# Folding the weights' sign into a parametric relu of slope -2^32, in a top-k attention kernel with two feed-forward layers

## The chip, the core and the metric

The program runs on one core of a Trainium2 chip. The metric is the device time of one execution in microseconds (us), lower is better. The core has five engines that work side by side, each through its own queue in a fixed order: PE (TensorE, the matrix multiplier), DVE (VectorE), ACT (ScalarE), POOL (GpSimd) and SP (SyncE), which here only issues DMA transfers. They wait for each other through semaphores. TensorE's clock is granted in two levels, 1.2 and 2.4 GHz; the profile shows it as a share of full speed (0.5 or 1.0, and means between).

## The reference, cut to what matters

```python
# q, k, v: (4, 8, 576, 64) float32
scores = q @ k.T / 8
kth    = 32nd largest of each row                       # top_k = 32
attn   = softmax(where(scores >= kth, scores, -1e9))
x      = (attn @ v), heads side by side                  # (2304, 512)
x = (sigmoid(x @ w_gate) * (x @ w_val)) @ w_out          # 512 -> 1536 -> 512
out = relu(x @ w_in)**2 @ w_out2                         # 512 -> 2048 -> 512
```

The five weight matrices come as 64-bit floats, q, k and v as 32-bit floats.

## The kernel before, in words

**Work.** The 2304 tokens are 18 blocks of 128. Chunks 0 to 5 are one block each, chunks 6 to 11 two blocks. For each chunk the attention runs in units: one block and one head, so 8 units a block and 144 in all. A unit named `_1_4` is block 1, head 4. Its scores are made on PE (`sp`), copied to SBUF by ACT (`S`), ranked on DVE (four MAX8 and three MATCH_REPLACE, `mx` and `W`), turned into weights by ACT (lines 419 and 421 or 435) with small steps on POOL (`bs`, `dg`), transposed on PE (`tp`, `tq`), copied by ACT (`PT`, `PE`), multiplied with the values on PE (`xp`) and, for two heads at a time, copied by ACT into the layers' input (`x_plain` for chunks 0 and 1). When a chunk's four such copies are there, its feed-forward layers run: `pg` (gate and value), `acc` (w_out), `ph` (w_in), `acc` (w_out2). Chunks 0 and 1 run them in plain 32-bit floats (function moe32, lines 907 to 1000); the later ones use two 16-bit halves of each weight and three matmuls for each product.

**Weights.** [...] A weight matrix is cut into raw blocks of 128 rows by 512 columns (`wg_r`, `wv_r`, `wo_r`, `wi_r`, `w2_r`; the page prints the last as `w_r`), each read as pairs of 32-bit words, and two of them make one tile `wg_c`, ..., `w2_c` (printed `w_c`). There are 68 raw blocks in 34 pairs. A 64-bit float's high word holds sign, 11 exponent bits and 20 mantissa bits. Read as a 32-bit float and multiplied by 2^-112 (REBIAS) by ACT at line 619, it has an exponent that fits 8 bits after the shift left by 3 that DVE does at line 621 on the whole pair. The shift pushes the sign out. The low word's top bits are made by ACT at line 625 (`low`), and POOL adds them in at line 635. The sign is put back in one of two ways, by pair: for every third pair (SGN, SGNS) ACT writes it into the low word at line 628 as the sign of a 16-bit float, so that POOL's add carries it in; for the other two thirds DVE takes the sign bit of the high word and ors it into the tile at line 632. That is 24 instructions at line 628 (12 pairs) and 44 at line 632 (22 pairs).

**Order.** No engine's order is written by hand. The program gives each step a priority (a time along an axis: `tw` for weight steps, `ta` for attention, `tm` for the layers) and a scheduler, which keeps its own estimate of durations, sets each engine's order from priorities and dependencies. In the first 120 us the attention of chunks 0 and 1 and the weights' conversion are interleaved on every engine. Raw blocks and converted tiles share a pool of 35 slots (WSLOTS); DMA issues all stand in SP's queue, where a transfer that has to wait for a slot or for a source holds up those behind it.

The lines that the change touches, all of them in conv, and what calls it:

Of the kernel before, what the change touches and what calls it, by code (L numbers as in the profile page):

```python
# [8 lines left out]
F16 = mybir.dt.float16  # L9
BF16 = mybir.dt.bfloat16  # L10
F32 = mybir.dt.float32
# [3 lines left out]
AF = mybir.ActivationFunctionType  # L15
ALU = mybir.AluOpType
# [31 lines left out]
SM2 = ()  # L48
XUP = 1000
DIAG = 2  # L50
SGN = 3
SGNS = (1,)
M4RAW = 0
KEYS1 = 1
GRAM = {2: ("wg",), 3: ("wv",), 5: ("wo",), 9: ("wi",), 13: ("w2",)}
# [3 lines left out]
MUP = 200.0  # L59
WSLOTS = 35  # L60
PREF = 4
YMOD = 0
LOP = 3
LOA = 0
TCI = 6
# [12 lines left out]
def tile_topk_attention__then__two_moe_layers(  # L78
# [14 lines left out]
    nc = tc.nc  # L93
# [464 lines left out]


    REBIAS = float(2.0**-112)  # L560
    weights = {"wg": w_gate, "wv": w_val, "wo": w_out, "wi": w_in, "w2": w_out2}
    order = ["wg", "wv", "wo", "wi", "w2"]
    pairs_of = {}
# [4 lines left out]
    raws = {}  # L568
    fetched = [0]
    live = [0]  # L570
    nblk = [0]
    flat = {}
    sums = {}
    parts = {}
# [3 lines left out]
    def fetch_to(i):  # L578
        while fetched[0] < len(blocks):
            b = fetched[0]  # L580
            spare = b >= len(blocks) - M4RAW
            if b > i and not (b <= i + PREF and (spare or live[0] + 3 <= WSLOTS)):
                break
            n, kt, fb = blocks[b]
            src = weights[n][kt * P : (kt + 1) * P, fb * 512 : (fb + 1) * 512]
            pool, kw = (mpool, {"tag": "m4", "bufs": M4}) if spare else (wpool, {"tag": "w"})
            if src.dtype == F32:
                t = pool.tile([P, 512], F32, name=f"{n}_r{kt}_{fb}", **kw)
                nc.sync.dma_start(t, src)
            else:  # L590
                t = pool.tile([P, 512, 2], U32, name=f"{n}_r{kt}_{fb}", **kw)
                nc.sync.dma_start(t.rearrange("p f t -> p (f t)"), src.bitcast(U32))
            if not spare:
                live[0] += 1
            raws[(n, kt, fb)] = t
            fetched[0] += 1

    def conv(name, pi):

        pr = pairs_of[name][pi]  # L600
        fetch_to(blocks.index((name, *pr[-1])))
        if (name, pi) in CM4:
            c = mpool.tile([P, 2, 512], F32, tag="m4", bufs=M4, name=f"{name}_c{pi}")
        else:
            c = wpool.tile([P, 2, 512], F32, tag="w", name=f"{name}_c{pi}")
            live[0] += 1
        rs = [raws.pop((name, kt, fb)) for kt, fb in pr]
        ci = c.bitcast(U32)
        wide = weights[name].dtype != F32
        for e, r in enumerate(rs):  # L610
            nblk[0] += 1
            if not wide:
                nc.gpsimd.tensor_copy(c[:, e], r)
            elif YMOD and nblk[0] % YMOD == 0:
                nc.gpsimd.tensor_scalar(
                    c[:, e], r.bitcast(F32)[:, :, 1], REBIAS, 1.0, op0=ALU.mult, op1=ALU.mult
                )
            else:
                nc.scalar.activation(c[:, e], r.bitcast(F32)[:, :, 1], AF.Copy, scale=REBIAS)
        if wide:  # L620
            nc.vector.tensor_scalar(ci, ci, 3, None, op0=ALU.logical_shift_left)
            for e, r in enumerate(rs):
                hi = r[:, :, 1]
                low = r[:, :, 0].bitcast(I32)
                nc.scalar.activation(low, r[:, :, 0], AF.Copy, scale=float(2.0**-29))
                if nblk[0] // 2 % SGN in SGNS:

                    nc.scalar.activation(
                        r.bitcast(F16)[:, :, 1], hi.bitcast(F32), AF.Copy, scale=float(2.0**-60)
                    )  # L630
                else:
                    nc.vector.scalar_tensor_tensor(
                        ci[:, e], hi, 0x80000000, ci[:, e], op0=ALU.bitwise_and, op1=ALU.bitwise_or
                    )
                nc.gpsimd.tensor_tensor(
                    c.bitcast(I32)[:, e], c.bitcast(I32)[:, e], low, op=ALU.add
                )
        live[0] -= sum(blocks.index((name, *b)) < len(blocks) - M4RAW for b in pr)
        for e, (kt, fb) in enumerate(pr):
            flat[(name, kt, fb)] = (c, e)  # L640
# [43 lines left out]
    def weight_step(n=1):  # L684
        for _ in range(min(n, len(steps) - nstep[0])):
            name, pi = steps[nstep[0]]
            conv(name, pi)
            nstep[0] += 1
# [649 lines left out]
```

## Time and profile before

| | us |
|---|---|
| median of 3 runs | 1262.75 |
| lowest, highest run | 1257.21, 1265.05 |
| the profiled execution, own time | 1259.55 |
| its span, first to last instruction | 1257.6 |
| PE busy in the span | 1164.5 (93%) |
| DVE, POOL, ACT busy | 951.2, 845.8, 832.5 |

The page has one execution. Its span begins with the first instruction; 1.95 us of its own time lie outside. PE is busy 93% of the span, but the 40 slices of the page are not alike: PE's share is low in the first tenth and near full from then on, while ACT, DVE and POOL are busiest in that first tenth. So the views have to be read by stretch, and the stretch from about 33 us, where the weights' conversion begins, to about 120 us, where chunk 0's layers begin, is told apart from the rest.

### The profile page before, as it was taken

The page shows a single profiled execution, that of the slowest core. Times are in us where ns is not written, and L with a number is a line of the kernel's source. Part 1 is how long each engine was busy: PE and PEld are TensorE (multiplying, and loading weights), DVE is VectorE, ACT ScalarE, POOL GpSimd, SP SyncE. Part 2 cuts the span into 40 slices and gives each one's busy share as a digit, 9 for nine tenths or more (in the row PEclk, how much of TensorE's full clock was granted, in tenths as well). Part 3 has the DMA queues.
Part 4 walks back from the last instruction along what each step waited for, and adds up shares of the span by engine and source line. Part 5 has one row for each costly group of instructions (what it writes and reads, how often), then busy time and mean ns, then how long its engine had stood idle before and what let it go on. Part 6 is the DMA issues. An engine that isn't in the chain of part 4 may idle for free. (4 is left out here: it accounts for less than half of the span.)

```text
span 1257.6 us, 30621 instructions
## 1 busy us (share of the span) xinstructions
PE 1164.5 (93%) x11477; PEld 949.1 (75%) x11477; DVE 951.2 (76%) x1965; ACT 832.5 (66%) x1719; POOL 845.8 (67%) x1294
## 2 busy tenths in 40 slices
PE   7653999999989979999999999999999999999998
PEld 5543887897877967878788778877886887787775
DVE  5998889789989988998899879998889969210010
ACT  4999987577878767876777766776567657323122
POOL 1698765467888577886877887787678659515233
PEclk9655999999999989999999999999999999999999
DMA  6988872123445466664677574656434523300000
GB/s 168 341 310 268 263 251 78 46 73 92 117 139 137 111 129 153 156 126 100 139 166 142 127 163 106 152 119 146 85 69 98 120 54 59 55 2 1 18 1 17
DMA packets 243188, 153.92 MB, mean 122 GB/s; under 512 B 193120, under 2 KB 209504, under 8 KB 243040
## 3 DMA queue, kind: packets, MB, share of 16 engines
q1 hardware_dynamic: 243040, 151.97, 48.2%
q8 instruction: 90, 1.47, 0.5%
q14 instruction: 58, 0.48, 0.1%
HBM read 105.51 MB, written 18.09 MB: 98 GB/s over the span
## 5 line engine op out<-in xcount | busy, mean ns | idle before, releaser
L393 DVE MAX8 mx<-W 128x8 f32<-128x576 f32 x432 | 327.7, 759 | 10.6
L394 DVE MATCH_REPLACE8 W<-mx,W 128x576 f32<-128x576 f32 x288 | 213.9, 743 | 0.0
L863 PE MATMUL ph<-x,wi_w 128*128 128x256 f16 (+1 forms) x1920 | 190.7, 253 | 7.3 <-ACT x L837 5.8
L884 PE MATMUL acc<-w_w,rh 128*128 128x512 f16 x768 | 182.2, 379 | 0.3 <-POOL rh L876 0.3
L863 PEld LDWEIGHTS <-wi_w 128*128 128x128 f16 x1920 | 156.7, 99 | 32.7 <-issue 8.3
L758 PE MATMUL pg<-xs,wg_w 128*128 128x256 f16 (+1 forms) x1440 | 147.4, 252 | 0.0
L758 PE MATMUL pv<-xs,wv_w 128*128 128x256 f16 (+1 forms) x1440 | 141.3, 251 | 2.6 <-DVE th L770 1.5
L382 PE MATMUL sp<-kst,qt 128*128 128x288 f32 x608 | 129.0, 326 | 12.4 <-DMA kst<-ks 7.4
L465 POOL TENSOR_TENSOR pp<-S,pp 128x512 f16<-128x512 f32 x192 | 137.1, 736 | 1.9
L419 ACT ACTIVATE S<-S,mx 128x576 f32<-128x576 f32 x144 | 111.8, 776 | 33.4 <-DVE mx L393 32.5
L758 PEld LDWEIGHTS <-wg_w 128*128 128x128 f16 x1440 | 117.8, 98 | 17.0 <-issue 0.7
L770 DVE TENSOR_TENSOR th<-pv,th 128x512 f32<-128x512 f32 (+1 forms) x60 | 34.7, 578 | 125.3 <-PE pv L758 118.1
L798 PEld LDWEIGHTS <-wo_w 128*128 128x128 f16 x1440 | 117.7, 98 | 14.6 <-issue 2.5
L758 PEld LDWEIGHTS <-wv_w 128*128 128x128 f16 x1440 | 117.1, 98 | 15.4 <-issue 3.4
L884 PEld LDWEIGHTS <-rh 128*128 128x128 f16 x768 | 72.3, 98 | 72.4 <-POOL rh L876 0.5
L385 ACT COPY S<-sp 128x576 f32<-128x576 f32 x144 | 92.0, 639 | 46.4 <-PE sp L382 39.9
L393 DVE MAX8 mx<-S 128x8 f32<-128x576 f32 x144 | 107.3, 745 | 20.1 <-ACT S L385 20.0
L463 POOL TENSOR_SCALAR S<-S,bs 128x576 f32<-128x576 f32 x96 | 71.9, 748 | 58.9 <-ACT pp L462 58.5
L394 DVE MATCH_REPLACE8 W<-mx,S 128x576 f32<-128x576 f32 x144 | 106.9, 742 | 0.0
L382 PEld LDWEIGHTS sp<-kst,qt 128*128 128x128 f32 x608 | 89.8, 192 | 21.8 <-DMA kst<-ks 7.5
L798 PE MATMUL acc<-gh,wo_w 128*128 128x256 f16 (+1 forms) x1104 | 104.6, 247 | 1.0 <-POOL gh L774 0.9
L875 POOL TENSOR_TENSOR r<-r 128x512 f32<-128x512 f32 (+1 forms) x80 | 70.2, 878 | 51.5 <-ACT rh L874 50.5
(246 smaller groups left out, 2315.5 us busy)
## 6 DMA issues: line engine op xcount, KB each, us to landing
kst<-ks SPq DMA_DIRECT2D x112, 288.0 KB, 3.1
v<-vd SPq DMA_DIRECT2D x32, 320.0 KB, 3.2
qn<-in_q_dram SPq DMA_DIRECT2D x128, 64.0 KB, 2.3
wi_r<-in_moe_w_in_dram SPq DMA_DIRECT2D x16, 512.0 KB, 7.0
w_r<-in_moe_w_out_dram SPq DMA_DIRECT2D x16, 512.0 KB, 5.2
v<-in_v_dram SPq DMA_DIRECT2D x56, 128.0 KB, 2.5
wg_r<-in_moe_w_gate_dram SPq DMA_DIRECT2D x12, 512.0 KB, 6.0
wv_r<-in_moe_w_val_dram SPq DMA_DIRECT2D x12, 512.0 KB, 6.3
```

The costliest lines, as they stand in the source:

```text
L382: nc.tensor.matmul(sp[:, e, 0:HALF], l, r, start=(x == 0), stop=(x == len(ops) - 1))
L385: nc.scalar.copy(ss.rearrange("p (e s) -> p e s", e=2), sp[:, :, 0:HALF])
L393: return nc.vector.max(m8, st.cur).ins
L394: ins = nc.vector.match_replace(st.wk, m8, st.cur, NEG).ins
L419: nc.scalar.activation(wk, wk, AF.Prelu, bias=kth, scale=-1.0, alpha=1.0 / BIG)
L463: nc.gpsimd.tensor_scalar(wk, wk, rz, 1.0, op0=ALU.mult, op1=ALU.mult)
L465: nc.gpsimd.tensor_tensor(pp[:, o : o + e - f], wk[:, f:e], pp[:, f:e], op=ALU.subtract)
L758: nc.tensor.matmul(pp[:, e * N : (e + 1) * N], wblk(wd, a, c, f0, P), xs[:, b_, c, :], start=(e == 0 and n == 0), stop=(n == 3 * KM - 1), ...
L798: nc.tensor.matmul(accs[d // 2][:, (d % 2) * N : (d % 2 + 1) * N], wblk("wo", a, f, d * P, P), gh[:, b_, e * N : (e + 1) * N], start=(f == ...
L863: nc.tensor.matmul(ph[:, e * N : (e + 1) * N], wblk("wi", a, c, f0, P), x2[:, b_, c, :], start=(e == 0 and n == 0), stop=(n == 3 * KM - 1) ...
L875: nc.gpsimd.tensor_tensor(r, r, r, op=ALU.mult)
L884: nc.tensor.matmul(acc2[i][:, 0:DM], gh[:, b_, e * N + i * P : e * N + (i + 1) * P], wblk("w2", a, f, 0, DM), start=(f == 0 and x == 0), s ...
```

## The change

ACT's scaling at line 619 becomes a parametric relu: for a negative input the result is multiplied by -2^32 as well. The value is then positive, and its exponent is larger by 32, which is one more bit above the eight that the shift keeps; the shift left by 3 carries that bit to the place of the sign. So the sign comes through the shift, and both ways of putting it back, lines 628 and 632, are gone. The numbers of instructions at lines 619, 621, 625 and 635 stay. An unused way of scaling on POOL (YMOD, which was 0) goes too.

```diff
-SGN = 3
-SGNS = (1,)
...
     REBIAS = float(2.0**-112)
+    NEGBIT = -float(2.0**32)
...
         for e, r in enumerate(rs):
-            nblk[0] += 1
             if not wide:
                 nc.gpsimd.tensor_copy(c[:, e], r)
-            elif YMOD and nblk[0] % YMOD == 0:
-                nc.gpsimd.tensor_scalar(
-                    c[:, e], r.bitcast(F32)[:, :, 1], REBIAS, 1.0, op0=ALU.mult, op1=ALU.mult
+            else:
+                nc.scalar.activation(
+                    c[:, e], r.bitcast(F32)[:, :, 1], AF.Prelu, scale=REBIAS, alpha=NEGBIT
                 )
-            else:
-                nc.scalar.activation(c[:, e], r.bitcast(F32)[:, :, 1], AF.Copy, scale=REBIAS)
         if wide:
             nc.vector.tensor_scalar(ci, ci, 3, None, op0=ALU.logical_shift_left)
             for e, r in enumerate(rs):
-                hi = r[:, :, 1]
                 low = r[:, :, 0].bitcast(I32)
                 nc.scalar.activation(low, r[:, :, 0], AF.Copy, scale=float(2.0**-29))
-                if nblk[0] // 2 % SGN in SGNS:
-
-                    nc.scalar.activation(
-                        r.bitcast(F16)[:, :, 1], hi.bitcast(F32), AF.Copy, scale=float(2.0**-60)
-                    )
-                else:
-                    nc.vector.scalar_tensor_tensor(
-                        ci[:, e], hi, 0x80000000, ci[:, e], op0=ALU.bitwise_and, op1=ALU.bitwise_or
-                    )
                 nc.gpsimd.tensor_tensor(
                     c.bitcast(I32)[:, e], c.bitcast(I32)[:, e], low, op=ALU.add
                 )
```

Since a scheduler sets the order, the other instructions move as well. Lines after the change are smaller by up to 17: 619 becomes 611, 625 becomes 618, 552 becomes 549, 964 becomes 948.

ACT's queue ahead of the copy that completes chunk 0's input (`x_plain<-xp_0_3`, the last heads of block 0), before:

```order
L486 COPY PT_0_7_943<-tp_0_7_944 128x512
L495 COPY PE_0_3_855<-tq_0_7_950 64x128
L619 ACTIVATE wi_c0_1000<-wi_r0_0_890 128x512
L628 ACTIVATE wi_r0_0_890<-wi_r0_0_890 128x512
L619 ACTIVATE wi_c0_1000<-wi_r1_0_892 128x512
L625 ACTIVATE wi_r1_0_892<-wi_r1_0_892 128x512
L619 ACTIVATE wi_c1_1080<-wi_r2_0_982 128x512
L625 ACTIVATE wi_r2_0_982<-wi_r2_0_982 128x512
L419 ACTIVATE S_1_2_936<-S_1_2_936,mx_1_2_1060 128x576
L628 ACTIVATE wi_r1_0_892<-wi_r1_0_892 128x512
L552 COPY x_plain_324<-xp_0_3_953 128x128
```

and the same place now:

```order
L483 COPY PT_0_7_909<-tp_0_7_910 128x512
L492 COPY PE_0_3_825<-tq_0_7_916 64x128
L611 ACTIVATE wi_c0_964<-wi_r0_0_858 128x512
L618 ACTIVATE wi_r0_0_858<-wi_r0_0_858 128x512
L611 ACTIVATE wi_c0_964<-wi_r1_0_860 128x512
L618 ACTIVATE wi_r1_0_860<-wi_r1_0_860 128x512
L611 ACTIVATE wi_c1_1042<-wi_r2_0_948 128x512
L618 ACTIVATE wi_r2_0_948<-wi_r2_0_948 128x512
L549 COPY x_plain_318<-xp_0_3_919 128x128
```

The two sign steps are gone and line 419's step for unit `_1_2` stands earlier; in the whole queue ahead of this copy there are 39 scalings in both orders, and 14 sign steps before and none now.

SP's queue where the second weight matrix (`wv`) is fetched, before:

```order
L592 DMA wv_r2_0_462<-in_moe_w_val_dram 128x1024
L592 DMA wv_r3_0_464<-in_moe_w_val_dram 128x1024
L592 DMA wv_r0_1_476<-in_moe_w_val_dram 128x1024
L155 DMA kn_1_0_726<-in_k_dram 128x4x64 x2
L592 DMA wv_r1_1_478<-in_moe_w_val_dram 128x1024
```

and now:

```order
L589 DMA wv_r2_0_452<-in_moe_w_val_dram 128x1024
L589 DMA wv_r3_0_454<-in_moe_w_val_dram 128x1024
L152 DMA kn_1_0_700<-in_k_dram 128x4x64 x2
L589 DMA wv_r0_1_464<-in_moe_w_val_dram 128x1024
L589 DMA wv_r1_1_466<-in_moe_w_val_dram 128x1024
```

One weight block (`wv_r0_1`) has gone behind the fetch of keys `kn_1_0`, which waits for a slot that PE frees.

PE's queue where chunk 0's second layer begins (`ph_0_0`, on w_in), before:

```order
L939 MATMUL acc1_0_1261<-g_0_5_1672,wo_c5_986 128x128 x8
L483 MATMUL tp_1_6_1968<-dg_1_6_1934,S_1_6_1541 128x128 x4
L382 MATMUL sp_2_2_2109<-kst_2_2_0_1951,qt_2_1_0_1963 128x288
L494 MATMUL tq_1_6_1975<-dg_1_6_1934,S_1_6_1541 64x128
L964 MATMUL ph_0_0_1810<-x_plain_324,wi_c0_1000 128x128 x2
```

and now:

```order
L541 MATMUL xp_1_1_1508<-PE_1_1_1384,v_1_1_0_725 64x128 x2
L339 MATMUL qpt_2_0_1764<-ident_81,qn_2_0_1481 128x128 x2
L948 MATMUL ph_0_0_1742<-x_plain_318,wi_c0_964 128x128 x2
L948 MATMUL ph_0_0_1742<-x_plain_318,wi_c1_1042 128x128 x2
...
L948 MATMUL ph_0_1_1799<-x_plain_318,wi_c0_964 128x128 x2
L948 MATMUL ph_0_1_1799<-x_plain_318,wi_c1_1042 128x128 x2
L480 MATMUL tp_1_4_1772<-dg_1_4_1535,S_1_4_1116 128x128 x4
```

Chunk 0's second layer stands ahead of the transposes of units `_1_4` to `_1_6` and the scores of units `_2_0` to `_2_2`, which it followed before. From the first `pg` of chunk 2 on, PE's order is the one before but for a unit here and there.

## Rows read from the trace of the kernel before

**Rows 1.** Busy time by stretch: start, length, engines, granted clock, DMA share, GB/s.
```profile
32.00:63.00 31.00, 20.14 (x98) 15.25 (x96) 28.25 (x52) 29.96 (x53) 20.56 (x21) 0.63 0.94 340
33.00:120.00 87.00, 43.52 (x212) 33.52 (x211) 80.34 (x136) 83.75 (x149) 70.67 (x65) 0.58 0.86 306
...
126.00:157.00 31.00, 28.42 (x287) 26.15 (x287) 25.60 (x53) 29.17 (x55) 22.92 (x24) 1.00 0.81 264
...
283.00:1069.00 786.00, 759.14 (x8333) 619.52 (x8333) 698.26 (x1481) 561.56 (x1226) 601.92 (x1016) 0.99 0.54 120
```

**Rows 2.** PE's waits, 33 to 120 us: total, times, longest.
```profile
PE tp L483 <- DVE kn L176: 15.0, 1, 15.0
PE tp L483 <- ACT x_plain L552: 6.8, 3, 3.2
```

**Rows 3.** PE's waits, 126 to 1069 us.
```profile
PE sp L382 <- DMA kst<-ks: 7.4, 8, 1.7
PE acc L939 <- DVE g L929: 4.2, 2, 2.1
```

**Rows 4.** ACT and PE in order of time: start, duration, idle time before.
```profile
33.32 1.35 ACT L628 ACTIVATE wg_r<-wg_r 128x512 f16<-128x512 f32 x1
34.42 0.72 ACT L625 ACTIVATE wg_r<-wg_r 128x512 int32<-128x512 uint32 x1
...
118.70 1.34 ACT L628 ACTIVATE wi_r<-wi_r 128x512 f16<-128x512 f32 x1
120.07 0.27 ACT L552 COPY x_plain<-xp 128x128 f32<-128x128 f32 x1
...
122.31 2.34 PE L917 MATMUL pg<-x_plain,wg_c 128*128 128x128 f32 x10
```

**Rows 5.** ACT's sign steps alone (line 628), two stretches.
```profile
33.00:126.00 93.00, 18.95 (x14) 0.58 0.86 304
126.00:220.00 94.00, 13.40 (x10) 0.98 0.62 197
```

**Rows 6.** DVE's sign steps alone (line 632), the same stretches.
```profile
33.00:126.00 93.00, 19.53 (x26) 0.58 0.86 304
126.00:220.00 94.00, 11.69 (x18) 0.98 0.62 197
```

**Rows 7.** ACT's groups: busy, mean ns; idle before.
```profile
L419 ACT ACTIVATE S<-S,mx 128x576 f32<-128x576 f32 x144 | 111.8, 776 | 33.4 <-DVE mx L393 32.5
L462 ACT ACTIVATE pp<-S,bs 128x576 f16<-128x576 f32 x96 | 74.5, 776 | 42.9 <-issue 20.3 <-DVE bs L458 16.4 <-ACT qn L357 1.9
...
L619 ACT ACTIVATE wi_c<-wi_r 128x512 f32<-128x512 f32 x16 | 10.9, 685 | 0.1
```

**Rows 8.** POOL's adds (line 635), 33 to 120 us.
```profile
33.00:120.00 87.00, 54.38 (x37) 0.58 0.86 306
```

**Rows 9.** POOL and DVE in order of time.
```profile
33.63 0.30 POOL L416 TENSOR_SCALAR bs<-mx 128x1 f32<-128x1 f32 x1 [5.70 <-DVE mx L393]
...
41.03 2.54 POOL L635 TENSOR_TENSOR wg_c<-wg_c,wg_r 128x512 int32<-128x512 int32 x2 [0.94 <-DVE wg_c L621]
...
62.18 1.80 POOL L416 TENSOR_SCALAR bs<-mx 128x1 f32<-128x1 f32 x1
...
62.00 1.34 DVE L632 SCALAR_TENSOR_TENSOR wg_c<-wg_r,wg_c 128x512 uint32<-128x512 uint32 x2
```

**Rows 10.** SP's issues of weights and keys, and ACT's first use.
```profile
45.43 2.93 SPq L592 DMA_DIRECT2D wv_r<-in_moe_w_val_dram  x5
56.09 1.25 SPq L155 DMA_DIRECT2D kn<-in_k_dram  x2
...
59.76 0.65 ACT L619 ACTIVATE wv_c<-wv_r 128x512 f32<-128x512 f32 x1
```

**Rows 11.** Chunk 0's second layer on PE, and the last weight adds.
```profile
192.02 2.50 PE L964 MATMUL ph<-x_plain,wi_c 128*128 128x128 f32 x20 [0.47 <-ACT x_plain L957]
...
197.14 1.29 POOL L635 TENSOR_TENSOR w_c<-w_c,w_r 128x512 int32<-128x512 int32 x1
```

More of the change, by code (lines that the diff above doesn't have):

```diff
@@ L61 @@
 PREF = 4
-YMOD = 0
 LOP = 3
@@ L570, in tile_topk_attention__then__two_moe_layers @@
     live = [0]
-    nblk = [0]
     flat = {}
```

## The prediction

> **What bounds the kernel now.** I read the busy time by stretch first. PE has 1164.5 us of work in a span of 1257.6, so 93 us are its to lose, and the stretches say where they lie: in 33 to 120 us PE is busy 43.5 of 87 us, and with the clock at a mean of 0.58 even that work runs near half speed, whereas from 126 us on it is busy 28.4 of 31 us and from 283 to 1069 us 759 of 786 [rows 1]. After about 126 us the kernel is PE working through its queue; what can be had is in the stretch before, and the time at which PE's dense work begins.
>
> In that stretch ACT is busy 83.8 of 87 us (96%), DVE 80.3 (92%), POOL 70.7 (81%), the transfers' share is 0.86 [rows 1]. So ACT ends last, DVE is close behind. PE's waits there confirm the order: its two largest are on a DVE step of 15.0 us, which itself stands behind conversion steps, and on ACT's copies into the layers' input, 6.8 us [rows 2]. The list in order of time shows the hand-over: ACT's last sign step runs at 118.70, the copy that completes chunk 0's input at 120.07, and PE's run of `pg` starts at 122.31 [rows 4]. Everything on PE behind that point is queued in a fixed order, so if this copy comes N us earlier, the end comes about N us earlier, unless a later wait takes it back.
>
> **What the change removes.** ACT loses 14 of its sign steps in 33 to 126 us, all ahead of the copy at 120.07, and 10 behind it, 32.4 us busy in all [rows 5]. Busy times of neighbours overlap, so the price on a full ACT is the distance from one start to the next: 33.32 to 34.42, 1.10 us [rows 4]. 14 x 1.10 = 15.4 us. DVE loses 26 + 18 steps, 31.2 us, of them 19.5 in the stretch [rows 6]. In both orders the same 39 scalings stand ahead of that copy in ACT's queue, so nothing of the conversion is merely put off past it.
>
> **What it adds.** 68 scalings with Prelu in place of Copy; 39 ahead of the copy. No row before has Prelu with constants alone. The nearest has a per-row bias: 776 ns for 576 columns, and a Copy with a per-row scale takes the same 776 [rows 7], so it is the per-row operand, not the function, that makes those two longer than the 685 of line 619. I take 0. Bounds: if all of 776 - 685 = 91 ns were Prelu's, 39 x 0.091 = 3.5 us; a gain is excluded, because the elements and their stride stay. No function table is loaded: Prelu is in use already.
>
> **What the rest of the stretch lets through.** With 15.4 us off ACT, 87 us becomes 71.6. DVE would need 80.3 - 19.5 = 60.8: room. POOL needs 70.7 as it stands, so it would be as full as ACT was. But POOL's adds are now stretched by DVE: 37 of them take 54.4 us, 1.47 each [rows 8], and two in a row without disturbance 2.54, 1.27 each [rows 9]; 37 x 0.20 = 7.4 us are blocked time. While a pair of DVE sign steps ran at 62.00 to 63.34, a POOL step that takes 0.30 alone took 1.80 [rows 9]. Of DVE's steps that block so, the sign steps are 26 and the shifts 19, so I give back 26/45 of 7.4, 4.3 us: POOL needs about 66 of 71.6. A full lock would give more: the Trainium skill (SBUF — State Buffer, section "SBUF: two separate sides") calls the shared port pair an exclusive lock, held for the whole instruction, for GpSimd against a DVE instruction with two SBUF inputs. By that rule the 26 sign steps kept POOL out for up to 19.5 us, and POOL would need only some 51; the rows give at most 7.4 us of it on the adds, since DVE does most of the waiting, and I keep 66.
>
> The transfers are the other limit. At a share of 0.86, the stretch holds 0.86 x 87 = 75 us of transfers, so with no new idle time it can shrink by 12 us and not by 15. The five `wv` blocks issued at 45.43 are first used at 59.76, and the next issue comes at 56.09 [rows 10], so there is some ten us of slack in the first half to spend. In the new order `wv_r0_1` has gone behind `kn_1_0`, which waits on PE; its use comes later than 59.76, and PE's release comes earlier with all else, so I price this at 0, and at 3 us if the slack is used up.
>
> So the copy comes 15.4 us earlier by ACT alone, 12 by the transfers; I take **12**, the lower of the two. Bounds 3 (below) and 15.4.
>
> **After 120 us.** PE is the bound; ACT loses 13.4 and DVE 11.7 us more, but beside PE's work. What they can give is PE's two waits of 4.2 us on DVE's `g` step [rows 3]; I take 2, bounds 0 and 4.2. Chunk 0's second layer now comes ahead of three units of attention on PE. Before, it started at 192.02 with its weights long ready [rows 11]; with 12 us less in front and three units fewer (PE's 43.5 us in 33 to 120 us at a clock of 0.58 serve about nine units [rows 1], so by estimate 2.8 us each at full clock) it starts near 171. The last weight adds, at 197.14 before, have to be earlier by then too; they are behind 24 x 1.10 us less on ACT, so I price this at 0. From 283 us on PE's order is nearly the one before and its waits, 7.4 us on fetched keys the largest [rows 3], have nothing to do with the weights: 0.
>
> **Sum.** -12 - 2 + 0 = -14. Made against the profiled execution, 1259.55 - 14 = 1245.6. That execution lay 3.2 us under the median of 1262.75; from the median the same sum gives 1248.8. I forecast between the two, **1247 us**.
>
> **Rivals.**
>
> *The transfers or POOL take over early.* If weights arrive no faster than they did, ACT runs ahead and then waits. For it: the share is 0.94 in 32 to 63 us [rows 1], where 6% of 31 us is 2 us; against it: 0.86 over the whole stretch, and ACT shows no wait for a weight block now. Fully bound in the first third, where 2 us can go, and half bound in the rest, where at most 10 can, the gain is 3 to 7 us: about 1255. The Trainium skill gives a rate for this (SBUF — State Buffer, section "A bandwidth-pool intuition that's wrong (but worth ruling out)"): some 358 GB/s between HBM and one core, and that this door is almost always the end-to-end bottleneck. The trace has 340 GB/s in 32 to 63 us and 306 over the stretch, near it; by that figure alone, as an estimate, 306 x 87 / 358 = 74 us, a gain of at most 13. Chance 0.30.
>
> *Nothing comes of it.* The copy is earlier but the PE waits of the later chunks grow by as much, since DVE and POOL, at 698 and 602 of 786 us [rows 1], pace the attention there. Against it: in 283 to 1069 us PE idles only 27 us, most of it not on attention's ranking. Time 1257 to 1262. Chance 0.12.
>
> *Slower: PE meets weights that aren't there.* PE takes its queue in order, and chunk 0's second layer now stands some three units earlier. If weights come no sooner than before, the last of them at 197 us, PE arrives near 171 at a layer whose 128 matmuls take 16 us (20 of them 2.50 [rows 11]), so that it stands for 10 us with the attention of blocks 1 and 2 queued behind it; and as in 33 to 120 us, where pauses go with a clock of 0.58 [rows 1], some 6 us of the work around the pause is at half clock and takes 6 more. 1259.55 + 10 to 16 = 1270 to 1276. It decides if the last adds on POOL come later than about 190 us. That they are behind less work on every engine speaks against it. Chance 0.06.
>
> *The change doesn't do what it says:* Prelu costs more on this strided read. The sign steps themselves show that ACT can take twice the time for a form, 1.35 against 0.72 us beside them [rows 4]; at that price 39 x 0.63 = 25 us would come back against 15 removed, 1270. The row with Prelu speaks against it [rows 7]. Chance 0.02.
>
> **How the numbers follow.** Forecast 0.50, its own range 1242 to 1252; the four rivals the other 0.50. The range leaves out the two slower cases and the tail of the best: its upper end holds the second rival's half, 1259; its lower end is the whole 15.4 and 4.2 with 3 of later waits, 1259.55 - 22.6 = 1237. A measurement of this kernel can tell about 1%, 12.6 us, from no change. The forecast's 14 is close to that, so I split its 0.50 into 0.44 faster and 0.06 within, and the first rival's 0.30 into 0.03 and 0.27: faster 0.47. The third and fourth rival are slower by over 1%: 0.08. Between lies the rest, 0.45.
>
> **What will show it.** Right, step by step: line 611 at 0.66 to 0.71 us; ACT's copy `x_plain<-xp_0_3` near 108 us and PE's run of `pg` near 110; ACT still above 93% busy up to there; POOL's adds at 1.35 us or less; the last adds before 185; PE's busy time the same 1164 us, less what half clock cost, and its idle time down by about 14. Wrong: ACT waiting for weight blocks or for POOL's `bs` in 40 to 105 us (first rival); the `pg` run early but PE's idle time after 126 us up by 10 (second); a PE wait at `ph` or `acc` on weight tiles (third).

## The result, and the profile after

The changed kernel takes 1248.23 us (median of 7 runs, 1246.89 to 1255.64) against 1261.08 before: a ratio of 0.9906, 95% interval 0.988 to 0.9933, some 12 us. The profiled execution is the slowest of the seven, 1255.64 us with a span of 1253.9. A second profile of the same kernel, taken with the experiments, has 1249.41 and 1247.6, nearer to the median; where the two differ both are given, the second one as *again*.

Busy time by stretch after the change, with the columns of [rows 1]:

```profile
32.00:63.00 31.00, 22.63 (x115) 17.58 (x115) 28.90 (x56) 28.51 (x59) 22.05 (x26) 0.73 1.01 367
33.00:120.00 87.00, 53.04 (x301) 42.72 (x301) 68.58 (x128) 79.65 (x159) 71.18 (x76) 0.69 0.98 348
126.00:157.00 31.00, 31.00 (x317) 29.35 (x315) 21.45 (x53) 24.53 (x49) 24.80 (x27) 1.00 0.83 271
283.00:1069.00 786.00, 758.35 (x8239) 618.04 (x8238) 686.00 (x1458) 549.01 (x1205) 588.57 (x1000) 0.98 0.53 119
```

In the same 87 us PE does 53.04 us of work where it did 43.52; the transfers' share has gone from 0.86 to 0.98, DVE from 80.3 to 68.6, and ACT from 83.8 to 79.7. From 126 to 157 us PE has no pause left. But from 283 to 1069 us it is busy no more than before, at a slightly lower mean granted clock (0.98 for 0.99). Rows in order of time after the change, answering to [rows 4] and [rows 11]:

```profile
107.42 0.27 ACT L549 COPY x_plain<-xp 128x128 f32<-128x128 f32 x1
...
109.55 2.15 PE L901 MATMUL pg<-x_plain,wg_c 128*128 128x128 f32 x10
...
164.72 2.94 PE L948 MATMUL ph<-x_plain,wi_c 128*128 128x128 f32 x24 [0.33 <-ACT x_plain L941]
...
172.45 2.54 POOL L619 TENSOR_TENSOR w_c<-w_c,w_r 128x512 int32<-128x512 int32 x2
```

The copy that completes chunk 0's input is 12.65 us earlier, `pg` 12.8. Chunk 0's second layer starts 27 us earlier and waits for no weight. The scalings with Prelu, and POOL's adds in 33 to 120 us, answering to [rows 7] and [rows 8]:

```profile
L611 ACT ACTIVATE wi_c<-wi_r 128x512 f32<-128x512 f32 x16 | 10.9, 684 | 0.0
```

```profile
33.00:120.00 87.00, 56.66 (x43) 0.69 0.98 348
```

A scaling takes what it took, 684 ns for 685. An add takes 56.66 / 43 = 1.32 us, for 1.47. PE's largest waits in 126 to 1069 us, answering to [rows 3]:

```profile
PE ph L847 <- ACT x L821: 7.0, 2, 3.9
PE acc L782 <- POOL gh L758: 3.0, 3, 1.7
PE sp L379 <- DMA kst<-ks: 3.0, 3, 1.2
...
PE acc L923 <- DVE g L913: 1.8, 2, 1.5
```

The wait on `g` has shrunk from 4.2 to 1.8 us, that on fetched keys from 7.4 to 3.0. In their place stand waits in and behind chunk 2's layers: on `gh`, and on `x`, once at chunk 2's `ph` (3.9 us) and once at chunk 3's (3.1, where the kernel before waits 3.85 too). About half of what the lead then loses goes there. Two places where every kernel here has done the same work on PE (34 units' scores at the first, 53 at the second) show it: the first `pg` of chunk 2 and the first `ph` of chunk 3. Before, after and again:

```profile
319.81 0.39 PE L758 MATMUL pg<-xs,wg_w 128*128 128x128 f16 x4
...
449.07 6.03 PE L863 MATMUL ph<-x,wi_w 128*128 128x128 f16 x72 [3.85 <-ACT x L837]
```

```profile
305.17 0.94 PE L742 MATMUL pg<-xs,wg_w 128*128 128x128 f16 x14
...
445.44 5.81 PE L847 MATMUL ph<-x,wi_w 128*128 128x128 f16 x72 [3.10 <-ACT x L821]
```

```profile
302.74 0.94 PE L742 MATMUL pg<-xs,wg_w 128*128 128x128 f16 x14
...
438.92 5.81 PE L847 MATMUL ph<-x,wi_w 128*128 128x128 f16 x72 [3.00 <-ACT x L821]
```

The lead is 14.6 us (again: 17.1) at the first place and 3.6 (again: 10.2) at the second; from there on it stays, 3.7 and 10.0 at the end of the spans. So 11 and 7 us of the lead are lost between these two rows, which lie 129.3 us apart before and 140.3 and 136.2 after. I call this distance the **chunk-2 stretch**.

### The profile page after: what moved, and what is told of

It reads as the page before. It is cut to its first block, busy times and chain, and to the rows that moved or that the text cites. A ratio compares the mean times of both kernels' runs of the same rounds, so it can differ in the third digit from the quotient of the medians.

```text
span 1253.9 us, 30560 instructions
## 1 busy us (share of the span) xinstructions
PE 1171.7 (93%) x11477; PEld 954.9 (76%) x11477; DVE 918.5 (73%) x1921; ACT 804.2 (64%) x1695; POOL 827.7 (66%) x1294
## 3 DMA queue, kind: packets, MB, share of 16 engines
q1 hardware_dynamic: 243040, 151.97, 48.0%
q8 instruction: 90, 1.47, 0.5%
## 5 line engine op out<-in xcount | busy, mean ns | idle before, releaser
L847 PE MATMUL ph<-x,wi_w 128*128 128x256 f16 (+1 forms) x1920 | 194.0, 256 | 8.6 <-ACT x L821 8.6
L847 PEld LDWEIGHTS <-wi_w 128*128 128x128 f16 x1920 | 160.3, 101 | 33.5 <-issue 9.0
L742 PE MATMUL pv<-xs,wv_w 128*128 128x256 f16 (+1 forms) x1440 | 144.7, 254 | 1.1 <-DVE x2s L817 0.7
L379 PE MATMUL sp<-kst,qt 128*128 128x288 f32 x608 | 135.1, 333 | 8.2 <-ACT S L382 3.2
L379 PEld LDWEIGHTS sp<-kst,qt 128*128 128x128 f32 x608 | 92.3, 195 | 19.6 <-ACT S L382 4.1
```

The lines of the kernel that those rows point to most:

```text
L379: nc.tensor.matmul(sp[:, e, 0:HALF], l, r, start=(x == 0), stop=(x == len(ops) - 1))
L742: nc.tensor.matmul(pp[:, e * N : (e + 1) * N], wblk(wd, a, c, f0, P), xs[:, b_, c, :], start=(e == 0 and n == 0), stop=(n == 3 * KM - 1), ...
L847: nc.tensor.matmul(ph[:, e * N : (e + 1) * N], wblk("wi", a, c, f0, P), x2[:, b_, c, :], start=(e == 0 and n == 0), stop=(n == 3 * KM - 1) ...
```

## The experiments

All times in one table. *Copy* is the start of the copy that completes chunk 0's input, *pg* the first one of chunk 2; the order is PE's in the chunk-2 stretch, "old" where it is the kernel before's word for word and "new" where it is another, six different ones in all. The same PE instructions run in the stretch in every kernel, and the same number ahead of it. Ratios are to the kernel before, which had medians of 1257.93 to 1261.08 beside these runs. Copy, pg and stretch come from one profiled execution each.

| kernel | median us | ratio, 95% | copy | pg | chunk-2 stretch | order |
|---|---|---|---|---|---|---|
| before | | | 120.07 | 319.81 | 129.3 | old |
| changed | 1248.23 | 0.9906 (0.988 to 0.9933) | 107.42 | 305.17 | 140.3 | new |
| again | 1249.15 | 0.9919 (0.9904 to 0.9933) | 106.64 | 302.74 | 136.2 | new |
| ACT's part | 1262.87 | 1.0019 (1.0001 to 1.0037) | 112.11 | 320.28 | 139.9 | new |
| DVE's part | 1254.81 | 0.9964 (0.9947 to 0.998) | 116.92 | 311.16 | 130.0 | old |
| low words on DVE | 1245.09 | 0.989 (0.9871 to 0.991) | 104.12 | 301.34 | 136.3 | new |
| filled | 1248.28 | 0.992 (0.9902 to 0.9938) | 107.11 | 303.24 | 136.6 | new |
| before, unfilled | 1268.93 | 1.0085 (1.0065 to 1.0105) | 120.52 | 319.45 | 139.9 | new |
| low words, chunk 2 | 1240.2 | 0.9841 (0.9814 to 0.9868) | 107.09 | 302.00 | 135.2 | new |
| old order | 1243.4 | 0.9884 (0.9862 to 0.9906) | 106.72 | 304.56 | 130.6 | old |
| depth 2 | 1229.77 | 0.9769 (0.9748 to 0.9789) | 98.51 | 288.88 | 129.0 | old |
| four pairs kept | 1243.16 | 0.9874 (0.9851 to 0.9897) | 111.91 | 305.46 | 128.7 | old |
| before, depth 2 | 1248.25 | 0.9921 (0.9904 to 0.9938) | 111.68 | 310.46 | 130.1 | old |
| depth 2, low words on DVE | 1227.33 | 0.9747 (0.9724 to 0.977) | 94.23 | 287.64 | 129.1 | old |

**Again.** The changed kernel as it is.

> The changed kernel once more, for a second profiled execution. In the first one the copy that completes chunk 0's input came 12.7 us earlier than before, but only 3.9 us of that reached the end: PE idled 2.7 us more in 200 to 283 us and 7 us more in 283 to 400 us, with the clock at 0.83 in 340 to 380 us. If that loss belongs to the one execution, this profile has its span at 1245 to 1249 us, the copy again at 107 to 108, and a clock of 0.97 or more in 340 to 380. If it belongs to the new order of instructions, PE's waits on ACT's x and POOL's gh in 300 to 400 us come back at 7 us together, the clock falls there again, and the span is 1252 to 1255. The ratio to the kernel before is 0.988 to 0.993 either way.

The ratio is 0.9919. The greater part of the late loss came back, 7 us of it, with the same waits; 4 us of the first profile's 11 belong to that execution, and why it lost them stays open. The copy, at 106.64, is earlier than the 107 to 108 expected. So the loss is the new order's or the early PE's; the experiments after the first four tell these apart.

**ACT's part alone.** In conv, the function that rebuilds a weight as a 32-bit float, pairs counted from 1:

```diff
+        fold = npair[0] % 3 == 1
...
+                if not fold:
+                    nc.vector.scalar_tensor_tensor(
+                        ci[:, e], r[:, :, 1], 0x80000000, ci[:, e], op0=ALU.bitwise_and, op1=ALU.bitwise_or
+                    )
```

(Prelu where `fold` holds, Copy elsewhere.)

> Prelu for the 12 pairs whose sign ACT put back, so that ACT's 24 sign steps are gone; the other 22 pairs keep Copy and DVE's 44 sign steps. My theory (ACT's 14 sign steps ahead of the copy set PE's start): the copy at 106 to 110 us as in the changed kernel, time 1247 to 1251, ratio 0.988 to 0.994. Rival one (DVE's sign steps are the limit, or become it at once: 26 of them by 0.75 us remain in the stretch): DVE's 80 us of work up to there don't shrink, the copy comes at 115 to 119, time 1256 to 1261, ratio 0.995 to 1.0.

Neither: the copy is 8 us earlier, between the two ranges, and nothing of it reaches the end. Ahead of it stand 37 scalings here, not 39. Stretch of 33 to 110 us with ACT's part alone, the largest of PE's waits in 110 to 283 us, and its Copy and Prelu scalings side by side in one execution (in this kernel line 619 is Copy and line 615 Prelu):

```profile
33.00:110.00 77.00, 40.29 (x203) 31.70 (x202) 73.87 (x129) 64.09 (x127) 60.92 (x58) 0.61 0.89 312
```

```profile
PE acc L933 <- DVE g L923: 8.2, 3, 4.8
```

```profile
L619 ACT ACTIVATE wi_c<-wi_r 128x512 f32<-128x512 f32 x10 | 6.7, 672 | 0.0
...
L615 ACT ACTIVATE wi_c<-wi_r 128x512 f32<-128x512 f32 x6 | 3.9, 680 | 0.0
```

ACT has come down to 64.1 of 77 us, and DVE, with its sign steps, stands at 73.9, 96%: it is the bound now, and ACT's last wait ahead of the copy, 3.35 us at 104.03, is on DVE's `mx`. Behind the copy PE waits 8.2 us on DVE's `g`, where it was 4.2, and at chunk 2's `pg` the lead is gone (320.28 for 319.81). The chunk-2 stretch, in an order of its own, then takes 10.6 us more; of the 11.1 us that it is behind there, 6.5 come back later (span 1262.2 for 1257.6). Prelu takes 8 ns a step more than Copy here; by matrix it is 3 less to 8 more in this kernel and 6 to 18 more in the next, at most 0.7 us for 39 steps.

**DVE's part alone.** The same with the two kinds of pairs exchanged:

```diff
+        fold = npair[0] % 3 != 1
...
+                if not fold:
+                    nc.scalar.activation(
+                        r.bitcast(F16)[:, :, 1], r[:, :, 1].bitcast(F32), AF.Copy, scale=float(2.0**-60)
+                    )
```

> The other half of the change alone: Prelu for the 22 pairs whose sign DVE put back, so that DVE's 44 sign steps are gone; the other 12 pairs keep Copy and ACT's 24 sign steps. My theory: ACT stays as full as before, the copy at 118 to 121 us, time 1258 to 1262, ratio 0.997 to 1.002; what there is of gain is PE's waits on DVE's g, 0 to 4 us. Rival one (DVE): the copy at 108 to 112, ratio 0.99. In between, 113 to 117, would say that each engine's sign steps hold the other up, ACT's wait for POOL and DVE counting as well as its own work.

The copy is at 116.92, 3.2 us earlier, at the edge of the band that speaks for each engine holding up the other (13 of ACT's sign steps stand ahead of it, one fewer than before). The stretch of 33 to 110 us:

```profile
33.00:110.00 77.00, 39.47 (x184) 30.44 (x183) 62.85 (x111) 76.26 (x139) 55.21 (x61) 0.78 0.89 313
```

ACT is busy 99% of it: its wait of 2.1 us on POOL's `bs` is gone, and ACT alone bounds. Behind the copy the lead grows to 8.7 us. DVE has 18 sign steps less beside the layers there, and PE's wait on `g` is 2.8 us for 4.2; that this is the whole reason isn't shown. With the old order at chunk 2 7.9 us of the lead are kept there, and 5.0 at the end. So my theory, that ACT's sign steps alone set PE's start, fell. The parts bring 8.0 and 3.2 us at the copy, and -0.5 and 8.7 at chunk 2's `pg`; together 12.7 to 13.4 and 14.6 to 17.1. At `pg` the whole is more than its parts: either engine takes over when the other is relieved (DVE at 96%, ACT at 99% above).

**Low words on DVE.**

```diff
+        ldve = npair[0] % 3 == 1
...
             for e, r in enumerate(rs):
+                if ldve:
+                    nc.vector.scalar_tensor_tensor(
+                        ci[:, e], r[:, :, 0], 29, ci[:, e],
+                        op0=ALU.logical_shift_right, op1=ALU.bitwise_or,
+                    )
+                    continue
```

> The changed kernel, but for every third pair the low word's top three bits are put in by one DVE step for each block (shift right by 29, or), in place of ACT's low step and POOL's add; the low word is truncated there instead of rounded. Ahead of the copy ACT has 15 low steps and 3 scalings less, 18 by 0.68 = 12 us. If ACT is still the limit of the changed kernel, the copy comes at 95 to 97 us and the time falls by another 8 to 12 us, ratio 0.979 to 0.984. If the transfers are (their share is 0.97 in 33 to 110 us in the changed kernel), the copy can come only as much earlier as 3 fewer blocks and the 3 per cent allow, 4 to 6 us: at 101 to 104 us, ACT shows waits on weight blocks, and the ratio is 0.985 to 0.989.

12 us of ACT's work are gone, and the copy, at 104.12, is only 2.5 to 3.3 us earlier than in the changed kernel. The stretch of 33 to 105 us, and ACT's last wait ahead of the copy:

```profile
33.00:105.00 72.00, 36.62 (x210) 27.28 (x211) 65.04 (x124) 61.01 (x124) 45.53 (x52) 0.68 0.98 347
```

```profile
98.32 0.78 ACT L416 ACTIVATE S<-S,mx 128x576 f32<-128x576 f32 x1 [2.67 <-DVE mx L390]
```

ACT is busy 61.0 of 72 us, so it no longer sets the copy. What does is not settled: the transfers are full, 0.98, but DVE, with 12 low-word steps ahead of the copy, is busy 65.0 of 72 us, 90%. ACT's one wait for a weight block is 0.3 us, where the case of the transfers had waits on weight blocks; it waits on DVE's `mx` (5.8 us) and PE's `tp` (3.0) instead, which speaks for DVE. The kernel's median is 4 us below *again*, with overlapping intervals.

**Filled, and before unfilled.** Between chunk 2's `x2pq` and its `ph` PE's queue had attention before:

```
L830 MATMUL x2pq_2_4334<-x2_2_4333,ones_86 128x128
L544 MATMUL xp_4_1_4432<-PT_4_2_4261,v_4_1_0_3337 64x64
...
L382 MATMUL sp_4_7_4555<-kst_4_7_1_4408,qt_4_3_1_4256 128x288 x2
...
L863 MATMUL ph_2_0_4355<-x2_2_4333,wi_w0_2998 128x128
```

and has none now:

```
L814 MATMUL x2pq_2_4266<-x2_2_4265,ones_86 128x128
...
L847 MATMUL ph_2_0_4287<-x2_2_4265,wi_w0_2930 128x128
```

One line moves it, in both kernels:

```diff
         lead = LEAD if ci < PRE0 else LEAD2
+        lead += 1 * (ci == 2)
```

> The changed kernel with the attention called one unit earlier beside chunk 2's layers (one line; PE's order up to chunk 2's first pg is that of the changed kernel word for word). In the changed kernel nothing stands on PE between chunk 2's x2pq and its ph, where the kernel before has the scores of two units and a product with the values; there and in the layer ahead PE waits. From the first pg of chunk 2 to the first ph of chunk 3 the same work takes 140.3 and 136.2 us in the two profiles of the changed kernel, 129.3 before. In this kernel five pieces of attention stand between x2pq and ph again. My theory (the order there gives back 7 to 11 us of the lead): the stretch takes 129 to 132 us, the time is 1242 to 1246, ratio 0.985 to 0.989. The rival (PE, being earlier, only meets the pace of the other engines there, whatever the order): the stretch stays at 135 to 140, time 1247 to 1251, ratio 0.990 to 0.993.

> The kernel before with the same line: PE's order up to chunk 2's first pg is the old one word for word, but here the line moves the pieces of attention away from between x2pq and ph, as the change did. My theory: the stretch from chunk 2's first pg to chunk 3's first ph grows from 129.3 to 135 to 140 us, with waits of ph on ACT's x, and the time is 6 to 10 us above the kernel before, ratio 1.004 to 1.008. The rival (only a PE that is early loses there): the stretch stays at 128 to 131, ratio 0.998 to 1.002.

The kernel before loses 10.7 us in the chunk-2 stretch by the line alone, with everything ahead of it unchanged (pg at 319.45). So an order can cost this without an early PE; 8.6 us of it are left at the end of the span. But the changed kernel doesn't get it back: 136.6 us. PE's waits in the filled kernel from 303 to 440 us:

```profile
PE x2pq L814 <- ACT x L812: 4.5, 4, 2.1
PE vn L215 <- ACT vs L206: 3.3, 1, 3.3
...
PE ph L847 <- ACT x L821: 1.3, 1, 1.3
```

The waits of `ph` on `x` have gone from 6.4 us (again: 3.4 at chunk 2's `ph`, 3.0 at chunk 3's) to 1.3 at chunk 3's alone, and `x2pq`, one step ahead in the same chain, waits 4.5 instead. Filling that one gap moved the wait; my theory was right about the order and wrong about the gap.

**Low words, chunk 2.** Low words on DVE, and the line with another number:

```diff
+        lead += -2 * (ci == 2)
```

> The kernel with a third of the low words on DVE (the low word truncated there instead of rounded), with the attention called two units later beside chunk 2's layers, so that three other pieces stand between x2pq and ph and PE has one unit less ahead of them. Copy that completes chunk 0's input at 103 to 105 us as without the line. My theory: if the stretch from chunk 2's first pg to chunk 3's first ph falls from 136.3 to 130 to 132 us, the time is 1239 to 1242 and below all others; the rival (the pace of the other engines) has it at 135 to 138 and the time at 1244 to 1247.

The stretch is 135.2, as the rival has it, though attention stands between `x2pq` and `ph` here; the time, 1240.2, is in my theory's range all the same. The kernel runs in another order further on as well (its lead is 5.8 us at chunk 4's `ph` and 15.4 at chunk 5's, with other pieces of attention done), so its time decides nothing on the stretch. The copy came later than expected. Low words on DVE, then this kernel:

```profile
104.12 0.27 ACT L549 COPY x_plain<-xp 128x128 f32<-128x128 f32 x1
```

```profile
107.09 0.27 ACT L549 COPY x_plain<-xp 128x128 f32<-128x128 f32 x1
```

Up to the copy every engine of the two kernels has the same instructions in the same order; their executions part by 3 us between 41 and 48 us and stay so. A copy can thus differ by 3.0 us from one execution to the next, and neither the 2.5 to 3.3 us of the low words nor the 3.2 us of DVE's part stands clear of that.

**Old order.** DVE's part, and ACT's for the first 21 pairs:

```diff
+        fold = npair[0] <= 21 or npair[0] % 3 != 1
```

> The change for the first 21 of the 34 pairs and for every pair that DVE served; five late pairs (the 22nd, 25th, 28th, 31st and 34th) keep Copy and ACT's sign steps, 10 in all. Every engine's order is that of the changed kernel word for word beyond the copy that completes chunk 0's input; from chunk 2's first pg to chunk 3's first ph PE's order is that of the kernel before, word for word. So it has the change's gain ahead of the copy and the old order at chunk 2, at the price of 10 late ACT steps that stand beside PE's work. My theory (the new order at chunk 2 costs 7 to 11 us): the copy at 106.5 to 107.5, chunk 2's first pg at 303 to 308, the stretch from there 129 to 131 us, time 1243 to 1247, ratio 0.986 to 0.990, below the changed kernel's. The rival (an early PE meets the pace of the other engines there): the stretch takes 135 to 139 and the time is 1250 to 1253.

As my theory had it: copy 106.72, pg 304.56, stretch 130.6, time 1243.4. This is the decisive run: a PE that is 15.3 us early at `pg` keeps 13.9 through the stretch and to the end of the span when its order there is the old one, though ACT has 10 steps more to do. In the median the old order is worth some 4 to 6 us (0.9884 for 0.9919 of *again*, where the intervals just touch). Busy time in the chunk-2 stretch of the kernel before, of *again* and of this kernel:

```profile
319.00:449.00 130.00, 119.58 (x1611) 103.33 (x1611) 117.14 (x266) 102.05 (x242) 95.94 (x169) 0.99 0.47 128
```

```profile
302.00:439.00 137.00, 122.57 (x1609) 106.05 (x1608) 115.88 (x265) 100.17 (x237) 92.29 (x167) 0.96 0.45 123
```

```profile
304.00:435.00 131.00, 120.61 (x1610) 104.69 (x1611) 117.00 (x266) 101.99 (x241) 94.91 (x168) 0.98 0.46 127
```

PE idles 14.4 us in the new order, 10.4 in the old, early or not, and needs 2 to 3 us more for the same matmuls, at a clock of 0.96 for 0.98 and 0.99. Over all fourteen profiles the old order has 128.7 to 130.6 us and the six others 135.2 to 140.3, whatever the lead. Where PE has the old order, ACT, DVE and POOL have theirs in the stretch too, and where it has another, so have they; so what is shown is the order of all four engines together, not that of PE's queue alone.

**Depth 2.** One line, in the changed kernel and in the kernel before:

```diff
-PREF = 4
+PREF = 2
```

> The changed kernel with every sign folded, but weight blocks fetched only two ahead of their use instead of four. It too has PE's old order from chunk 2's first pg to chunk 3's first ph; its front is ordered otherwise, with 34 scalings ahead of the copy in place of 39. My theory: the stretch takes 129 to 131 us, with the copy at 104 to 110 and the time at 1242 to 1248. The rival: the stretch takes 135 to 139, time 1248 to 1254. If the shallower fetch leaves the transfers idle in 33 to 105 us, their share falls below 0.9 and the copy is later than 110.

> The kernel before, its sign steps as they were, with weight blocks fetched two ahead instead of four; PE has the old order at chunk 2. The changed kernel with this depth took 1229.77 us, with its copy at 98.5. What part of that is the depth alone? My theory (the sign steps fill ACT here too; 36 scalings and 12 sign steps stand ahead of the copy in place of 39 and 14): the copy at 111 to 115, the stretch at chunk 2 129 to 131, time 1248 to 1254, ratio 0.990 to 0.996, so that the change is worth about 20 us at this depth, where the new order at chunk 2 doesn't come with it. The rival (the depth does it, by fetching keys and queries sooner): the copy at 100 to 106, time 1236 to 1243.

The changed kernel takes 1229.77 us, the kernel before 1248.25: with the old order at chunk 2 in both, the change is worth 18.5 us. The stretch came as my theory had it in both; the changed kernel's copy and time lie below every range that I gave, and its share in 33 to 105 us is 0.95, so the shallower fetch doesn't leave the transfers idle. The two copies at depth 2:

```profile
98.51 0.27 ACT L549 COPY x_plain<-xp 128x128 f32<-128x128 f32 x1
```

```profile
111.68 0.27 ACT L552 COPY x_plain<-xp 128x128 f32<-128x128 f32 x1
```

13.2 us apart, as at depth 4. The depth itself brings 8 to 9 us at the copy in either, with 5 scalings fewer ahead of it in the changed kernel and 3 scalings and 2 sign steps fewer in the kernel before. In the changed kernel the lead grows on behind the copy, from 21.6 us to 30.9 at `pg`, in the kernel before only from 8.4 to 9.4; why is not separated.

**Four pairs kept.** Copy and ACT's sign steps in pairs 1, 10, 19 and 28, Prelu in all others:

```diff
+        fold = npair[0] % 9 != 1
```

> The change for 30 of the 34 pairs; the 1st, 10th, 19th and 28th keep Copy and ACT's sign steps. 6 of these 8 steps stand ahead of the copy that completes chunk 0's input, with the same 39 scalings as in the changed kernel; at chunk 2 PE has the old order. If ACT sets the copy in the changed kernel, 6 by 1.10 us = 6.6 us come back and the copy is at 113 to 114. If the transfers set it and ACT has slack (it is busy 92 per cent of 33 to 105 us there), the copy is at 108 to 111. Time by the theory of the order, with the stretch at 129 to 131: 1247 to 1251 in the first case, 1244 to 1247 in the second.

The copy is at 111.91, between the two cases: 6 steps put it back by 4.5 to 5.3 us, 0.75 to 0.88 each and not 1.10. So in the changed kernel ACT is at its limit, and something else close to it: work added to ACT costs most of its price, work taken away (low words on DVE) brings a fourth of it at most. Of the later copy hardly anything reaches chunk 2's `pg`: 305.46, for 305.17 and 302.74. The time, 1243.16, is below the changed kernel's though it does more work. At the end of the chunk-2 stretch it is 14.9 us ahead of the kernel before, where *again* is 10.2; at the end of the spans it is 19.2 ahead, for 10.0, in another order further on as well.

**Depth 2, low words on DVE.** Both edits, with other pairs than above:

```diff
-PREF = 4
+PREF = 2
...
+        ldve = npair[0] % 3 == 2
```

> The changed kernel with the depth of two, and with the low word of every third pair put in by DVE (truncated there instead of rounded) in place of ACT's low step and POOL's add; PE has the old order at chunk 2. 31 scalings and 21 low steps ahead of the copy, where the changed kernel at this depth has 34 and 34. If ACT still sets the copy at this depth (busy 68 of 72 us), 16 steps by 0.68 = 11 us go: the copy at 88 to 91, time 1219 to 1223, ratio 0.968 to 0.972. If the transfers set it (share 0.95), 3 blocks fewer at 331 GB/s are worth 4.7 us: the copy at 93 to 96, time 1224 to 1228.

The copy, at 94.23, and the time lie where the case of the transfers has them. The stretches of 33 to 94 us, which ends with the copy, and of 33 to 105 us:

```profile
33.00:94.00 61.00, 41.99 (x208) 32.19 (x208) 59.14 (x115) 52.76 (x107) 37.59 (x46) 0.83 0.97 338
33.00:105.00 72.00, 51.29 (x285) 41.02 (x285) 67.38 (x130) 62.11 (x127) 44.19 (x54) 0.86 0.95 331
```

ACT has 8 of 61 and 10 of 72 us of slack. But up to the copy DVE is as full as the transfers, 59.1 of 61 us (97%) beside a share of 0.97, and ACT's largest wait in 33 to 105 us is on DVE's `mx` (3.8 us); which of the two sets the copy is not separated. With 1227.33 us it is the lowest here, 30.6 below the kernel before beside it, but its interval overlaps that of depth 2, so the low words are not shown to help there.

## Why the prediction was right, and where it was not

The forecast of 1247 us came to lie 1 us from the median, in part by luck: two terms were off in opposite directions. The lead at chunk 2's `pg`, for which the sum has 14 us, was 14.6 and 17.1; the order behind it, for which the sum has 0, took back 11.0 and 6.9.

*ACT ahead of the copy, 12 by the lower of two limits:* right in size, 12.65 and 13.4. The four kept pairs show ACT's limit. The low words on DVE show that ACT isn't the only one; that the other is the transfers is not shown. Their share is 0.97 up to the copy in the changed kernel, near the full one that the sum took, but in both runs with low words DVE is about as full as they are. That DVE is close behind ACT was said, but the sum gave the removal of its sign steps no share in the copy. ACT's part alone shows that it has one: where they stay, the copy comes 8 us earlier and not 12.

*"If this copy comes N us earlier, the end comes about N us earlier":* held for the change as far as `pg` (12.65 and 13.4 at the copy, 14.6 and 17.1 there), but not as a rule: 8.0 us at the copy are -0.5 at `pg` in ACT's part, 3.2 are 8.7 in DVE's, 8.2 are 14.4 with four pairs kept. The copy is one wait on PE's way, not the measure of its lead.

*Prelu at nothing:* right, 680 for 672 ns in one execution, and 684 for 685. The working put the 91 ns between 776 and 685 down to a per-row operand and left out that the longer rows have 576 columns and the shorter 512. In the kernel before ACT's copies from PE's output take 639 ns for 576 columns (L385) and 587 for 512 (L486), so by this estimate the columns make up more than half; that the rest is the operand's no run here separates.

*POOL's adds given back by DVE's sign steps:* right. 33 adds took 47.8 us in 33 to 110 us before, 1.45 each; with DVE's signs kept (ACT's part) 44.1 for 32, 1.38; with them gone (DVE's part) 43.4 for 34, 1.28. POOL has 71.2 us of work in the 87 after, for 43 adds in place of 37. DVE's own shifts were helped as well, from 1.14 us each in 33 to 120 us (19 of them) to 0.90 (22), which the sum left out. The whole lock that the Trainium skill states (SBUF — State Buffer, section "SBUF: two separate sides") could by the 26 DVE sign steps of [rows 6] have cost POOL up to 19.5 us on 37 adds, 0.53 each, as an estimate. The runs show 0.10 (between the two parts) to 0.17, which is below that bound and doesn't decide whether the lock is whole.

*PE's waits on `g`, 2:* the lead grew by 2.0 and 3.6 us between copy and `pg`. In ACT's part alone those waits doubled instead, which shows that DVE's steps behind the copy count too.

*Second layer near 171, last adds before 185, no wait on weights:* 164.7 and 172 to 175; the third rival didn't occur. The layer was 6 us earlier than estimated; the estimate turned PE's busy time into full-clock time by a mean clock, which the last section shows to be no measure of it.

*"From 283 us on PE's order is nearly the one before ...: 0":* this step failed. It priced a difference of order at nothing by its look. It is not the old one "but for a unit here and there": in the chunk-2 stretch all four engines run in another order, and that costs 7 us there (11 in the first profile), by waits along the chain `acc`, `x2pq`, `x`, `ph` (idle 14.4 us for 10.4) and by 2 to 3 us more of PE's busy time at a lower clock. *Old order* and *before, unfilled* settle that it is the order and not PE's earliness. The second rival (later waits eat it) thus held for 40 to 75 per cent of the lead, but by another cause than the one it named: DVE and POOL are not busier there, 115.9 and 92.3 us for 117.1 and 95.9. Which piece of that order costs how much is not settled; the filled kernel shows that it isn't the one gap.

*PE busy the same, idle down by 14:* busy is up, 1171.7 and 1170.1 us for 1164.5, so 6 to 7 more; idle 82.2 and 77.5 for 93.1, so 10.9 and 15.6 less.

The first rival's mechanism may be what stands next, the transfers at a share of 0.97; but they, or DVE, take over at 12 to 13 us and not at 3 to 7.

## What to carry to other kernels

When two engines are both above 90 per cent of a stretch, price a change that relieves both as one thing: here the halves alone brought -0.5 and 8.7 us at chunk 2's `pg` and the two together 14.6 to 17.1. When a scheduler sets the order, compare the order of the bounding engine past the end of the edit too, and don't price a difference there at nothing: in this kernel a one-line shift of it cost 10.7 us in one stretch with no work added. Take the scatter of a mark from two executions with the same order before a gain is read from one: here the copy's was 3 us. A lead is best followed at places where all versions have done the same work; the end alone would have hidden a gain of 17 and a loss of 7.

## What the runs showed of the hardware that I had not expected

The mean granted clock of a stretch in which PE is half idle says little of the work there. In 33 to 105 us PE has the same number of instructions, 176, in the kernel before and in DVE's part (PE's busy time alone):

```profile
33.00:105.00 72.00, 37.92 (x176) 0.57 0.90 324
```

```profile
33.00:105.00 72.00, 37.81 (x176) 0.80 0.93 330
```

37.9 us at a mean of 0.57 and 37.8 at 0.80. So the prediction's "even that work runs near half speed" was no conclusion to draw from such a mean; single rows do show the two levels (`pg`, ten matmuls, 2.15 us after, with a granted clock of 0.58 in 109.5 to 111.7 us, and 1.28 in *again*, at 1.00 in 108.0 to 109.3).

The transfers went past the 358 GB/s of the prediction: 367 in 32 to 63 us and 369 in 110 to 126, at a share of 1.01 and 1.04:

```profile
110.00:126.00 16.00, 16.00 (x154) 15.60 (x154) 12.18 (x25) 13.83 (x27) 13.46 (x15) 0.96 1.04 369
```

The Trainium skill (SBUF — State Buffer, section "A bandwidth-pool intuition that's wrong (but worth ruling out)") has some 358 GB/s between HBM and one core; the trace's figure counts all that the queues moved, which is more than HBM's part of it over the whole span (151.97 MB, of which 123.6 with HBM), so it agrees within what can be told here.
